# One softmax over both head groups for three of four batches, and a newly searched order of the first stage

## The chip, the core and the metric

The kernel runs on one core of a Trainium2 chip (trn2). The metric is the device time of one execution in microseconds; the kernel before took 826.61 us (median of 3 runs, 824.13 to 828.91).

## The reference

Three blocks follow each other. All inputs and the output are float32, but for the five weight matrices, which are float64.

```
# attention through 32 memory slots, 4 batches, 8 heads, 576 positions, head size 64
a      = softmax(phi over the 576 positions)           # [4,8,576,32]
k_m    = a^T k ;  v_m = a^T v                          # [4,8,32,64]
scores = q k_m^T / 8 ; attn = softmax(scores over 32)  # [4,8,576,32]
x      = (attn v_m) laid out as [2304, 512]
# first feed-forward block, 512 -> 2048 -> 512
x      = silu(x w_in) w_out
# second, 512 -> 1536 -> 512
out    = ((x w_a) * (x w_b)) w_out2
```

Nearly all products are made three times over: a float32 operand is split into a high part and a low part (what is left), and high by high, low by high and high by low are added up.

## The kernel before

**Stage one, 0 to about 131 us.** For each batch b the steps are: `weights` (L628), the softmax of phi up to its exp `ex`; `memory` (L655), 144 small products `kvp` of `ex` with k and v, their division `kvn` on ScalarE, and k_m transposed (`kt`, copied to `kT`); `values` (L700), v_m transposed (`vt`); `turn` (L709), q transposed, three turns of three 128x128 transposes (`qt`, copied to `qT` by ScalarE) for each of two head groups; and `scores` (L743), for each head group: eight products into the one `sc` tile, two VectorE transposes into `x`, the softmax over 32 slots (maximum, subtraction, exp on ScalarE, sum, division), a transpose back into `xt`, and the split of `xt` into the high part `at` (ScalarE) and the low part. `vw_first` (L873) folds v_m into w_in (`mp`, split into `m0` to `m3` by batch), so that the first product of the feed-forward block is `hp` = m times at, and the second `yp` = g times w_out with g = silu(hp). `tile_of` (L796) turns a float64 tile of w_in or w_out into float32 by integer operations. The feed-forward units of batches 0, 1 and half of 2 (`UNITS`, L910) run in this stage too, between the attention steps.

Each of these steps is a generator that says, by `op` (L531), which engine it needs, for how many ns by its author's table, after what, and which ring of buffers it takes. `run` (L571) plays that through: it takes the step of the lowest rank in the table `R` (L956) among those that can start, and issues it. So each engine gets a fixed order, in which it waits where its next instruction isn't ready. `keep_busy` (L236) puts products of ones, which nobody reads, into the bank about to be used, where the plan sees TensorE idle. The loads go out on SyncE's queue in the order of `LOADS` (L948): a name is the tensor, the batch and the head group (q20 is q of batch 2, head group 0; kv31 is k and v of batch 3, head group 1; wi and wo are tiles of w_in and w_out). A load waits until its buffer is free; q, kv and phi have two buffers each, weight tiles three, so the queue stands still behind a load that waits. `LOW_A` (L953) says how the low half of `at` is made, by batch: "V" is a subtraction on VectorE; "D" is a negated copy on ScalarE and a DMA from GpSimd that adds `xt`.

**Stage two, to about 405 us,** is the rest of the first feed-forward block, in the order of a scheduler that does not keep the program's order. **Stage three** is the second block in seven products a step (Strassen's scheme); its operands `yq` are split from y and from differences `T` of blocks of y (`sums`, L1092; `quarter_task`, L1110), in an order by the same `run`. PSUM has eight banks; each stage allocates pools of them, and the next stage's pools take the same banks: before, y and h's pools came first, then t (`bank`) and sc.

```
            t["x"] = p_s.tile([128, 2 * J, NM], F32, tag="x", bufs=2, name="x")
            t["xt"] = p_s.tile([128, 2, S], F32, tag="x", bufs=2, name="xt")
```

x and xt of a batch share that ring of two, so batch b + 1's scores can be taken into x only when batch b's x has been transposed.

Of the kernel before, what the change touches and what calls it, by code (L numbers as in the profile page):

```python
# [20 lines left out]
def attn_moe_moe2_kernel(  # L21
# [457 lines left out]
    ff["h"] = tc.alloc_tile_pool(name="ps_h", bufs=2, space=PSUM)
    ps_t = tc.alloc_tile_pool(name="ps_t", bufs=2, space=PSUM)  # L480
    ps_sc = tc.alloc_tile_pool(name="ps_sc", bufs=1, space=PSUM)
# [474 lines left out]
    R = dict(  # L956
        weights=(6, 55, 5, 16), memory=(26, 2, 43, 9), values=(46, 19, 22, 54), turn0=(38, 14, 15, 33),
        turn1=(24, 48, 41, 45), scores0=(7, 36, 47, 37), scores1=(23, 59, 28, 18), vw=(51, 53, 44, 49),
        first=(3,), m0=(4, 39, 11, 50), m1=(8, 32, 27, 35), wi=(12, 17, 31, 57), wo=(56, 1, 29, 21),
        units=(40,), g=(10,), y=(58,), late0=(20, 25, 34, 0), late1=(30, 52, 13, 42),  # L960
    )
# [385 lines left out]
```

## Time and profile before

| | us |
|---|---|
| median of 3 runs | 826.61 |
| the profiled execution | 829.91 |
| its span, first to last instruction | 828.1 |
| TensorE (PE) busy | 802.7, 97% of the span |
| VectorE (DVE) busy | 534.6, 65% |
| ScalarE (ACT) busy | 438.8, 53% |
| mean granted TensorE clock | 0.987 |

A granted clock of 1.00 is 2.4 GHz, 0.50 is 1.2 GHz, so the mean says how much of the span ran at half speed. PE's matmuls overlap, so its busy time is no measure of speed, but a gap in it is time in which no matmul ran.

### The profile page before, as it was taken

To read this page: it belongs to the slowest core of one execution; us is meant where nothing else is said; L and a number is where in the kernel's file an instruction comes from. 1 tells how busy PE (TensorE), PEld (TensorE's weight loads), DVE (VectorE), ACT (ScalarE), POOL (GpSimd) and SP (SyncE) were. 2 spreads that over 40 slices of the span, in tenths; PEclk is the share of its full clock that TensorE was granted. 3 is DMA by queue.
4 is the path that set the end of the run, shared out by engine and by line. 5 is a ranking of instruction groups with operands and counts; after the bars stand their busy time and mean duration, and the time that the engine had idled before them with its cause. 6 is when DMAs were issued, how large, how long until landed. Compare 5 with 4: busy or idle time off the path is not lost.

```text
span 828.1 us, 14335 instructions
## 1 busy us (share of the span) xinstructions
PE 802.7 (97%) x5696; PEld 737.4 (89%) x5696; DVE 534.6 (65%) x1050; ACT 438.8 (53%) x891; POOL 60.6 (7%) x75
## 2 busy tenths in 40 slices
PE   8888979999999999999999999999999999999997
PEld 5567869899999999999899999999999999999996
DVE  6887766656646665667698886568655685452534
ACT  4675677854654565667367765554424643222220
POOL 1000000100000000112001100110000100000000
PEclk9999999999999999999999999999999999999999
DMA  9757022432231232446397679877785975757753
GB/s 345 271 190 276 2 56 83 122 77 79 64 64 51 78 77 51 97 116 127 142 351 207 205 256 312 256 223 250 228 238 169 277 225 154 212 167 201 214 144 77
DMA packets 59027, 139.42 MB, mean 168 GB/s; under 512 B 5072, under 2 KB 30160, under 8 KB 58960
## 3 DMA queue, kind: packets, MB, share of 16 engines
q1 hardware_dynamic: 48448, 122.44, 44.2%
q0 software_dynamic: 9360, 15.54, 11.1%
q8 instruction: 45, 0.74, 0.4%
q10 hardware_dynamic: 1152, 0.52, 0.3%
q14 instruction: 22, 0.18, 0.1%
HBM read 101.71 MB, written 21.23 MB: 148 GB/s over the span
## 4 chain that ended last, share of the span: by engine, by line
PE 83%; DVE 1%; DMA 1%; ACT 0%; issue 0%
PE ab L69 31%; PE yp L69 22%; PE op L69 18%; PE hp L69 11%; PE mp L69 2%; DMA st_b<-in_moe_w_b_dram 1%; DVE yq L69 0%; DVE T L69 0%; ACT yq L69 0%; DVE y L69 0%; ACT y L69 0%; ACT u L69 0%; DVE e_a L78 0%; ACT e_b L78 0%
## 5 line engine op out<-in xcount | busy, mean ns | idle before, releaser
L69 PE MATMUL ab<-yq,wh 128*128 128x384 f32 x1080 | 260.3, 338 | 2.0 <-DVE yq L69 1.2
L69 PEld LDWEIGHTS ab<-yq,wh 128*128 128x128 f32 x1080 | 196.6, 189 | 9.2 <-DVE yq L69 1.5
L69 PE MATMUL ab<-yq,wl 128*128 128x384 f32 x432 | 146.1, 338 | 0.0
L69 DVE TENSOR_TENSOR gl<-g,gh 128x288 fp32r<-128x288 f32 x128 | 58.1, 455 | 66.6 <-ACT gh L69 66.4
L69 ACT ACTIVATE g<-hp 128x288 f32<-128x288 f32 x128 | 52.5, 410 | 86.7 <-PE hp L69 80.4
L69 ACT ACTIVATE u<-ab 128x384 f32<-128x384 f32 x108 | 52.4, 490 | 86.3 <-PE ab L69 85.7
L69 DVE TENSOR_TENSOR y<-op,y 128x512 f32<-128x512 f32 x54 | 37.3, 691 | 77.8 <-PE op L69 76.9
L69 PE MATMUL op<-wol,ph 128*128 128x512 f32 x216 | 85.4, 395 | 0.0
L69 PE MATMUL op<-woh,pl 128*128 128x512 f32 x216 | 85.1, 394 | 0.0
L69 PE MATMUL op<-woh,ph 128*128 128x512 f32 x216 | 84.3, 390 | 0.0
L69 PEld LDWEIGHTS ab<-yq,wl 128*128 128x128 f32 x432 | 81.5, 189 | 0.0
L69 DVE TENSOR_TENSOR u<-ab,u 128x384 f32<-128x384 f32 x108 | 59.8, 555 | 20.5 <-PE ab L69 19.5
L69 ACT ACTIVATE ph<-u 128x384 fp32r<-128x384 f32 x72 | 37.4, 524 | 67.0 <-DVE u L69 59.0
L69 DVE TENSOR_TENSOR y<-yp,y 128x288 f32<-128x288 f32 x104 | 47.3, 456 | 28.4 <-PE yp L69 28.2
L69 ACT ACTIVATE gh<-g 128x288 fp32r<-128x288 f32 x128 | 56.6, 443 | 3.1
L69 PEld LDWEIGHTS op<-woh,pl 128*128 128x128 f32 x216 | 40.5, 188 | 8.9
L69 PEld LDWEIGHTS op<-woh,ph 128*128 128x128 f32 x216 | 40.6, 188 | 6.7
L69 PEld LDWEIGHTS op<-wol,ph 128*128 128x128 f32 x216 | 40.5, 188 | 6.7
L69 PE MATMUL yp<-gh,wo_0h 128*128 128x288 f32 x128 | 39.0, 305 | 5.5 <-ACT y L69 4.5
L69 DVE TENSOR_TENSOR pl<-u,ph 128x384 fp32r<-128x384 f32 x72 | 39.2, 551 | 2.0 <-ACT ph L69 1.8
L69 PE MATMUL yp<-gh,wo_2h 128*128 128x288 f32 x128 | 38.9, 304 | 0.0
L69 PE MATMUL yp<-gl,wo_1h 128*128 128x288 f32 x128 | 38.2, 298 | 0.0
(175 smaller groups left out, 1734.9 us busy)
## 6 DMA issues: line engine op xcount, KB each, us to landing
yq<-yd SPq DMA_DIRECT2D x63, 768.0 KB, 4.5
yd<-yq SPq DMA_DIRECT2D x21, 768.0 KB, 4.3
st_wo<-in_moe_w_out_dram SPq DMA_DIRECT2D x16, 512.0 KB, 3.5
st_wi<-in_moe_w_in_dram SPq DMA_DIRECT2D x16, 512.0 KB, 5.1
st_a<-in_moe_w_a_dram SPq DMA_DIRECT2D x12, 512.0 KB, 5.3
st_b<-in_moe_w_b_dram SPq DMA_DIRECT2D x12, 512.0 KB, 5.3
wl<-s POOLq DMA_DIRECT2D x24, 256.0 KB, 5.8
st_o<-in_moe_w_out_dram SPq DMA_DIRECT2D x12, 512.0 KB, 6.0
```

Source lines behind the costliest of these rows:

```text
L69: ins = f(*a, **k)
```

## The change

For batches 1, 2 and 3 (`JOINT`), `scores` stops after its transposes into `x`, and a new generator `softmax` waits for both head groups and does each softmax operation once on [128, 36, 32] in place of twice on [128, 18, 32]; `split_at` then splits each head group's half of `xt`. The low half of batch 3 is made on VectorE. `LOADS`, the ranks `R` and the banks for `weights` and `turn` are new, found by a search over the plan (a load that the plan sees idle for over 1 us counts 1.5 us more in it, and `vw_first` waits in it for the batch before). The PSUM pools of all three stages are put in another order. In stage three, the first differences `T` get 1 us later in the plan.

```diff
+            if eng == "D" and at - free_at["D"] > 1000.0:
+                at += 1500.0
...
+        if b in JOINT:
+            if hg == 1:
+                add(R["soft"][b], softmax(b), free_at["T"])
+            return
...
+    def softmax(b):
+        yield op("V", 1370, [f"tx{b}0", f"tx{b}1"], take=("mxq", f"mxq{b}"))
+        x = st[b]["x"]
+        full = [128, 2 * J, NM]
+        mx = p_s.tile([128, 2 * J], F32, tag="mxq", bufs=2, name="mxq")
+        V.tensor_reduce(out=mx, in_=x, op=ALU.max, axis=AX.X)
+        yield op("V", 1360, free=[f"mxq{b}"])
+        V.tensor_tensor(out=x, in0=x, in1=mx.unsqueeze(2).to_broadcast(full), op=ALU.subtract)
+        yield op("A", 1180, table="exp")
+        A.activation(out=x, in_=x, func=AF.Exp, scale=scale)
+        yield op("V", 1900, take=("smq", f"smq{b}"))
+        sm = p_s.tile([128, 2 * J], F32, tag="smq", bufs=2, name="smq")
+        V.tensor_reduce(out=sm, in_=x, op=ALU.add, axis=AX.X)
+        V.tensor_scalar_add(sm, sm, EPS)
+        V.reciprocal(out=sm, in_=sm)
+        yield op("V", 1360, free=[f"smq{b}"])
+        V.tensor_tensor(out=x, in0=x, in1=sm.unsqueeze(2).to_broadcast(full), op=ALU.mult)
+        yield op("V", 1400, take=("x", f"xt{b}"), done=f"xt{b}", free=[f"x{b}"])
+        xt = st[b]["xt"] = p_s.tile([128, 2, S], F32, tag="x", bufs=2, name="xt")
+        V.transpose(out=xt.rearrange("p g s -> p (g s)"), in_=x.rearrange("p j m -> p (j m)"))
+        for g in range(2):
+            add(R["halves"][b], split_at(b, g), free_at["T"])
+    def split_at(b, g):
+        yield op("A", 680, [f"xt{b}"])
+        xt = st[b]["xt"][:, g]
+        hi, lo = at_hi[b][g], at_lo[b][g]
+        copy(A, hi, xt)
+        for o in low_half(LOW_A[b], 740, 680, hi, lo, xt, f"at{b}{g}0", f"xt{b}*2"):
+            yield o
...
-        "phi00 phi10 wo01 wo02 wi00 kv00 kv01 wi01 wi03 q01 wo00 q00 kv11 wi02 q11 kv10 q10 q21 q20 kv21 "
-        "phi20 kv20 wo03 kv30 kv31 q31 phi30 q30 "
+        "phi00 phi10 wi00 wo01 kv00 wo00 kv01 wi03 q00 wi01 q01 kv10 q11 kv11 wo03 phi20 q21 phi30 q10 kv21 "
+        "wi02 kv20 q31 q20 wo02 kv31 kv30 q30 "
...
-    LOW_A = ("V", "V", "V", "D")
+    LOW_A = ("V", "V", "V", "V")
...
+    JOINT = (1, 2, 3)
...
+        ps_o = mctx.enter_context(tc.tile_pool(name="ps_o", bufs=2, space=PSUM))
         ps_x = mctx.enter_context(tc.tile_pool(name="ps_x", bufs=WG, space=PSUM))
         ps_z = mctx.enter_context(tc.tile_pool(name="ps_z", bufs=WG, space=PSUM))
-        ps_o = mctx.enter_context(tc.tile_pool(name="ps_o", bufs=2, space=PSUM))
...
-            add(due_quarter(NS * tp + 2), sums(tp))
+            add(due_quarter(NS * tp + 2), sums(tp), 0.0 if tp else 1000.0)
```

The other pools move in the same way: stage one allocates t, h, sc, y in place of y, h, t, sc, and stage two m, h2, y2 in place of y2, h2, m. So `ps_x`, which stage three writes first, takes the banks of h2 and not those of y2.

**SyncE's loads, from the first q of batch 1 on.** `qq` is a load of q, `kv0` and `kv1` are the two buffers of k and v, `ph` is phi, `st_wo3` and `st_wi2` are weight tiles. Before (`qq_417` is q11, `qq_481` q10, `qq_575` q21, `qq_639` q20):

```order
L69 DMA qq_417<-in_q_dram 128x1x1152
L69 DMA kv1_116<-in_k_dram 128x2x576
L69 DMA kv1_116<-in_v_dram 128x2x576
L69 DMA qq_481<-in_q_dram 128x1x1152
L69 DMA qq_575<-in_q_dram 128x1x1152
L69 DMA qq_639<-in_q_dram 128x1x1152
L69 DMA kv0_115<-in_k_dram 128x2x576
L69 DMA kv0_115<-in_v_dram 128x2x576
L69 DMA ph_694<-in_phi_dram 128x4x288
L69 DMA kv1_116<-in_k_dram 128x2x576
L69 DMA kv1_116<-in_v_dram 128x2x576
L69 DMA st_wo3_752<-in_moe_w_out_dram 128x512
```

and with the change (`qq_391` is q11, `qq_558` q21, `qq_574` q10):

```order
L69 DMA qq_391<-in_q_dram 128x1x1152
L69 DMA kv1_116<-in_k_dram 128x2x576
L69 DMA kv1_116<-in_v_dram 128x2x576
L69 DMA st_wo3_450<-in_moe_w_out_dram 128x512
L69 DMA ph_478<-in_phi_dram 128x4x288
L69 DMA qq_558<-in_q_dram 128x1x1152
L69 DMA ph_562<-in_phi_dram 128x4x288
L69 DMA qq_574<-in_q_dram 128x1x1152
L69 DMA kv0_115<-in_k_dram 128x2x576
L69 DMA kv0_115<-in_v_dram 128x2x576
L69 DMA st_wi2_626<-in_moe_w_in_dram 128x2x256
L69 DMA kv1_116<-in_k_dram 128x2x576
```

The phi loads of batches 2 and 3 and tile 3 of w_out now stand ahead of q10. Before, q10 followed k and v of batch 1 at once, and phi of batch 3 stood near the end of the list, between its two q.

**ScalarE at the end of stage one,** around the split of batch 3's `at` and the copies of the last `yp` into y. Before:

```order
L69 ACTIVATE at_74<-xt 128x576
L69 ACTIVATE e_wi_0_1621<-st_wi_0_1440 128x512
L69 ACTIVATE g_1689<-hp 128x288
L69 ACTIVATE gh<-g_1689 128x288
L69 ACTIVATE at_82<-at_74 128x576
L69 ACTIVATE m3h<-mp 128x512
L69 ACTIVATE at_73<-xt 128x576
L69 ACTIVATE at_81<-at_73 128x576
L69 ACTIVATE m3h<-mp 128x512
L69 ACTIVATE y_123<-yp 128x288 x2
L69 ACTIVATE y_1732<-yp 128x288
```

and with the change:

```order
L69 ACTIVATE at_73<-xt 128x576
L69 ACTIVATE g_1634<-hp 128x288
L69 ACTIVATE gh<-g_1634 128x288
L69 ACTIVATE g_1647<-hp 128x288
L69 ACTIVATE gh<-g_1647 128x288
L69 ACTIVATE e_wi_0_1624<-st_wi_0_1482 128x512
L69 ACTIVATE at_74<-xt 128x576
L69 ACTIVATE y_123<-yp 128x288 x2
L69 ACTIVATE g_1714<-hp 128x288
L69 ACTIVATE g_1749<-hp 128x288
L69 ACTIVATE gh<-g_1714 128x288
L69 ACTIVATE gh<-g_1749 128x288
```

The two negated copies (`at_82<-at_74`, `at_81<-at_73`) are gone, `m3h` has moved ahead, and the last two copies into `y_123` no longer stand behind three `at` copies and two `m3h`.

**VectorE where stage three starts** (the `y` rows add stage two's last `yp` to y). Before:

```order
L78 ISA t_o_5246<-t_o_5246,e_o_5216 128x1024
L69 TENSOR_TENSOR y_1732<-yp,y_1732 128x288 x6
L69 TENSOR_TENSOR T_5428<-y_123 128x768
L69 TENSOR_TENSOR yq<-y_123,yq 128x768 x2
L69 TENSOR_TENSOR T_5440<-y_123,T_5428 128x768
L69 TENSOR_TENSOR T_5442<-y_123 128x768
```

and with the change:

```order
L78 ISA t_o_5214<-t_o_5214,e_o_5184 128x1024
L69 TENSOR_TENSOR y_1703<-yp,y_1703 128x288 x6
L69 TENSOR_TENSOR yq<-y_123,yq 128x768 x2
L69 TENSOR_TENSOR T_5406<-y_123 128x768
L69 TENSOR_TENSOR T_5408<-y_123,T_5406 128x768
L69 TENSOR_TENSOR T_5414<-y_123 128x768
```

The low halves of the first two operands `yq` now come ahead of the first difference `T`.

## Rows read from the trace of the kernel before

**Rows 1.** Stretches: length, busy us of PE, PEld, DVE, ACT, POOL; clock; DMA share; GB/s.
```profile
0.00:72.85 72.85, 61.23 (x871) 44.58 (x872) 58.42 (x120) 48.51 (x99) 3.27 (x10) 0.98 0.72 258
72.85:131.25 58.40, 51.06 (x538) 45.39 (x537) 36.96 (x77) 36.99 (x74) 1.87 (x2) 0.88 0.25 83
131.25:404.60 273.35, 273.34 (x2131) 260.11 (x2129) 169.54 (x362) 166.53 (x366) 23.42 (x27) 1.00 0.33 83
404.60:412.00 7.40, 5.54 (x21) 5.32 (x22) 7.33 (x9) 2.15 (x3) 0.00 (x0) 0.77 0.61 246
412.00:823.60 411.60, 411.44 (x2141) 382.06 (x2139) 261.65 (x484) 184.62 (x349) 32.09 (x36) 1.00 0.73 221
```

**Rows 2.** Timeline of PE at four places and where stage three starts: start, length, waits.
```profile
72.85 0.43 PE L69 MATMUL hp<-at,m1h 128*128 128x288 f32 x2
...
80.16 2.15 PE L69 MATMUL qt<-ident,qq 128*128 128x128 f32 x8 [2.74 <-DMA qq<-in_q_dram]
...
121.10 0.61 PE L69 MATMUL yp<-gh,wo_0h 128*128 128x288 f32 x1 [4.34 <-ACT y L69]
...
131.25 0.43 PE L69 MATMUL hp<-at,m3h 128*128 128x288 f32 x2
...
406.87 0.46 PE L69 MATMUL ab<-yq,wh 128*128 128x384 f32 x1 [1.23 <-DVE yq L69]
```

**Rows 3.** Timeline of ACT just before PE goes on at 121.10.
```profile
119.28 0.68 ACT L69 ACTIVATE at<-at 128x576 fp32r<-128x576 f32 x1
120.35 0.70 ACT L69 ACTIVATE y<-yp 128x288 f32<-128x288 f32 x2
```

**Rows 4.** Stretches of one us around two falls of the clock (columns as in rows 1).
```profile
21.00:22.00 1.00, 0.87 (x7) 0.80 (x7) 0.97 (x3) 0.53 (x3) 0.00 (x0) 1.00 1.05 415
...
23.00:24.00 1.00, 0.10 (x1) 0.00 (x0) 0.07 (x1) 0.77 (x2) 0.00 (x0) 1.00 1.04 389
...
25.00:26.00 1.00, 1.00 (x9) 0.67 (x8) 0.97 (x3) 0.65 (x3) 0.00 (x0) 0.50 1.05 390
...
80.00:81.00 1.00, 0.84 (x4) 0.87 (x5) 0.97 (x4) 0.00 (x0) 0.00 (x0) 0.50 1.03 410
```

**Rows 5.** The stretch 10 to 20 us, and the PE row that waited for v.
```profile
10.00:20.00 10.00, 8.29 (x166) 4.81 (x164) 8.87 (x16) 6.10 (x9) 0.00 (x0) 1.00 1.05 395
...
16.40 3.13 PE L69 MATMUL kvp<-kv,ex 64*32 64x192 f32 x136 [1.23 <-DMA kv<-in_v_dram]
```

**Rows 6.** Groups by line and shape up to 131.25 us: xcount | busy us, mean ns.
```profile
L69 DVE TENSOR_TENSOR x<-x,mxq 128x576 f32<-128x576 f32 x8 | 6.1, 757 | 0.2
...
L69 DVE TENSOR_TENSOR ex<-ph,bc 128x1152 f32<-128x1152 f32 x4 | 5.4, 1349 | 0.9 <-PE bc L69 0.9
...
L69 DVE STREAM_TRANSPOSE xt<-x 128x576 f32<-128x576 f32 x8 | 6.2, 776 | 0.2
...
L69 DVE TENSOR_TENSOR at<-xt,at 128x576 fp32r<-128x576 f32 x6 | 4.4, 736 | 0.0
...
L69 ACT ACTIVATE qT<-qt 128x384 f32<-128x384 f32 x24 | 11.1, 490 | 5.3 <-PE qt L69 5.2
...
L69 ACT ACTIVATE ex<-ex 128x1152 f32<-128x1152 f32 x4 | 4.7, 1164 | 0.6 <-DVE ex L69 0.6
```

**Rows 7.** Timeline of PE: products of ones, and attention products at full clock.
```profile
9.36 5.34 PE L69 MATMUL kvp<-ones 128*128 128x512 bf16 x24
...
93.40 3.15 PE L69 MATMUL kvp<-kv,ex 64*32 64x192 f32 x144
...
103.02 0.82 PE L69 MATMUL qt<-ident,qq 128*128 128x128 f32 x6
...
113.10 1.09 PE L69 MATMUL mp<-wi,vt 64*32 64x256 f32 x32
```

**Rows 8.** Timeline of DVE where stage three starts.
```profile
405.00 0.95 DVE L69 TENSOR_TENSOR T<-y 128x768 f32<-128x768 f32 x1
405.87 1.82 DVE L69 TENSOR_TENSOR yq<-y,yq 128x768 fp32r<-128x768 f32 x2
```

More of the change, by code (lines that the diff above doesn't have):

```diff
@@ L477, in attn_moe_moe2_kernel @@
     p_c = tc.alloc_tile_pool(name="p_c", bufs=1, side="right")
+    ps_t = tc.alloc_tile_pool(name="ps_t", bufs=2, space=PSUM)
+    ff["h"] = tc.alloc_tile_pool(name="ps_h", bufs=2, space=PSUM)
+    ps_sc = tc.alloc_tile_pool(name="ps_sc", bufs=1, space=PSUM)
     ff["y"] = tc.alloc_tile_pool(name="ps_y", bufs=2, space=PSUM)
[L479 to L481 removed]
     mm_pool[:] = ps_t, "t"
@@ L760, in scores @@
                 T.matmul(sc[o, par, :k], t["kT"][r, hg, o], qT[r, i0:i1, 32 * p : 32 * p + 32])
-        yield op("V", 150 + 780 * nj / J, [f"xt{b - 1}"] if b else [], take=("x", f"x{b}"), free=[f"sc{key}"])
+        yield op("V", 150 + 780 * nj / J, [f"xt{b - 1}"] if b else [], take=("x", f"x{b}"), done=f"tx{b}{hg}", free=[f"sc{key}"])
         if "x" not in t:
@@ L878, in vw_first @@
         yield op("T", 100 + 470 * len(halves), [f"vbd{b}"] + [f"wi{2 * hf + kc}" for hf in halves for kc in range(2)]
-                 + [f"{key}_0"] * halves[0], done=f"{key}_{halves[0]}", take=takes, rec=32 * len(halves))
+                 + [f"{key}_0"] * halves[0] + [f"m{b - 1}_{int(b == 1)}"] * (b > 0), done=f"{key}_{halves[0]}", take=takes, rec=32 * len(halves))
         cols = slice(256 * halves[0], 256 * halves[-1] + 256)
@@ L948, in attn_moe_moe2_kernel @@
     LOADS = (
-        "phi00 phi10 wo01 wo02 wi00 kv00 kv01 wi01 wi03 q01 wo00 q00 kv11 wi02 q11 kv10 q10 q21 q20 kv21 "
-        "phi20 kv20 wo03 kv30 kv31 q31 phi30 q30 "
+        "phi00 phi10 wi00 wo01 kv00 wo00 kv01 wi03 q00 wi01 q01 kv10 q11 kv11 wo03 phi20 q21 phi30 q10 kv21 "
+        "wi02 kv20 q31 q20 wo02 kv31 kv30 q30 "
     ).split()
     CUT = ()
-    LOW_A = ("V", "V", "V", "D")
+    LOW_A = ("V", "V", "V", "V")
     LOW_O = ("V", "V", "V", "V")
     BANKS = ("bank", "hp", "yp", "sc")
+    JOINT = (1, 2, 3)
     R = dict(
[L957 to L960, printed above, removed]
+        weights=(34, 57, 28, 60), memory=(26, 0, 7, 17), values=(54, 36, 35, 52), turn0=(49, 64, 30, 58),
+        turn1=(20, 12, 10, 48), scores0=(25, 39, 33, 4), scores1=(32, 56, 62, 41), vw=(24, 65, 53, 42),
+        first=(47,), m0=(40, 27, 43, 23), m1=(11, 21, 63, 16), wi=(15, 19, 61, 55), wo=(50, 37, 6, 66),
+        units=(51,), g=(8,), soft=(5, 29, 46, 13), halves=(45, 67, 14, 18), y=(22,), late0=(44, 59, 9, 31),
+        late1=(2, 38, 1, 3),
     )
-    BANK_W = ("yp", "yp", "yp", "yp")
+    BANK_W = ("yp", "hp", "bank", "hp")
     BANK_K = ("bank", "sc", "sc", "bank")
-    BANK_Q = ("bank", "yp", "yp", "hp")
+    BANK_Q = ("yp", "yp", "hp", "yp")
     fill()
@@ L988, in attn_moe_moe2_kernel @@
     pinned[0] = False
-    for p in (ps_sc, ps_t, ff["h"], ff["y"], p_c, p_s, p_in):
+    for p in (ff["y"], ps_sc, ff["h"], ps_t, p_c, p_s, p_in):
         p.release()
+    ps_m = tc.alloc_tile_pool(name="ps_m", bufs=2, space=PSUM)
+    ff["h"] = tc.alloc_tile_pool(name="ps_h2", bufs=3, space=PSUM)
     ff["y"] = tc.alloc_tile_pool(name="ps_y2", bufs=3, space=PSUM)
-    ff["h"] = tc.alloc_tile_pool(name="ps_h2", bufs=3, space=PSUM)
     p_y2 = ctx.enter_context(tc.tile_pool(name="p_y2", bufs=1, side="right"))
@@ L1017, in attn_moe_moe2_kernel @@
         tick()
-    for p in (p_g2, p_m2, ps_m, ff["h"], ff["y"], p_g, p_t, p_a):
+    for p in (p_g2, p_m2, ff["y"], ff["h"], ps_m, p_g, p_t, p_a):
         p.release()
```

1 line of the change is left out of this document (removed).

## The prediction

> **What bounds the kernel now.** I read the busy times by stretch first [rows 1]. From 131.25 us to 404.6 TensorE is busy for 273.34 of 273.35 us at a granted clock of 1.00, and from 412 to 823.6 for 411.44 of 411.60. The products there stay the same, so nothing can be gained in them: the other engines have room and would have to become much slower to be seen. Time can be won only in stage one, around 405 us, and in the end. Stage one has two parts. Up to 72.85 us, where the first `hp` of batch 1 stands [rows 2], TensorE waits for loads and for the softmax chain, and fills up with products of ones. From there to 131.25, the first `hp` of batch 3, it is idle for 58.40 - 51.06 = 7.34 us, and the mean clock is 0.88. The timeline of TensorE tells where [rows 2]: 2.74 us before a `qt` that waits for a load of q, and 4.34 us before a `yp` that waits for ScalarE's copy into y. What ScalarE did just before is in its own timeline [rows 3]: the negated copy of batch 3's `at` ran at 119.28, and the two copies out of `yp` that TensorE waited for came only after it, at 120.35. Behind such gaps the clock is at 0.50, 1.2 GHz, as in 80 to 81 us [rows 4]. A mean of 0.88 is 0.12 x 58.40 = 7.0 us of full-speed time not granted, of which I take 0.6 to have fallen into the idle time; 6.4 us were lost by slow products, 3.2 a gap. So the stretch holds 7.3 + 6.4 = 13.7 us of loss, and 58.4 - 13.7 = 44.7 us of work.
>
> **The two losses go.** With the change every `qt` stands ahead of the first `hp` of batch 1 in TensorE's order, the wait for q with it. The ScalarE copies into y follow one `at` copy, and the two negated copies, 0.68 us each [rows 3], don't exist. Neither place has anything left that TensorE would wait for, if the engines get there in time. That is 13.7 us less, against what the earlier part now costs.
>
> **The earlier part: more work ahead of the first hp of batch 1.** By the order, TensorE has done more by then: one more `kvp` set (3.15 us), two more sets of nine `qt` (0.82 for six, so 2.5 for both), one more `mp` (1.09), two more `sc` (half as many products each as `mp`, a little wider: 1.2), and eight more 128-column products of the `qt` kind at 0.14, 1.1, all by [rows 7]: 9.0 us together. The stretch after it shrinks by as much, to 44.7 - 9.0 = 35.7. If nothing else changed, the first `hp` of batch 1 would stand at 72.85 + 9.0 = 81.9.
>
> When will it stand there? I follow the chain that I take to set it. It begins with q10, which now has phi of batches 2 and 3 and a tile of w_out ahead of it. Up to and with it the queue holds 4 loads of phi, 5 of q, 8 of k or v (576 KB each, by the tiles' shapes) and 6 weight tiles (512 KB), 13.17 MB. The v that TensorE awaited at 16.40 [rows 5] ends 5.11 MB in both lists. The other 8.06 MB at 395 GB/s [rows 5] take 20.4 us: q10 lands at 36.8. Three transposes and three `qT` copies of 0.49 [rows 6] end at 38.7. ScalarE's exp of batch 0's second head group stands behind them, 0.68 by its sister of the same shape [rows 3]: 39.4. VectorE's sum, division and transpose back, with small operations between, take 3.0 [rows 6]: 42.4. The subtraction for `ex` of batch 2 follows (1.35), its exp (1.16) and a `qT` copy (0.49), after which TensorE gets its bank: 45.4. Five products of ones at 0.22, twelve `hp` products at 0.14, like `qt`'s, and the third `kvp` at 3.15 [rows 7] follow: 51.4, and VectorE's reciprocal ends at 51.9. From that one to the low half of batch 1's `at`, on which the first `hp` of batch 1 waits, VectorE has 49 instructions. Seven of 1152 columns at 1.35, one transpose of 1152 at 1.45 and two low halves of `at` at 0.74 make 12.4 us [rows 6]; the other 39, conversions of weights, score transposes, low halves of g, additions into y, cost 0.17 to 0.69 each in the same view, 17.5 together: 29.9. With 2 us of waits inside (for the last `kvp`, for ScalarE's half of w_out's tiles), an estimate, the first `hp` of batch 1 stands at 84.0, 2.1 us later than the 81.9.
>
> **The joint softmax** itself is nearly free of effect. Per head group the old form has four operations of 576 columns at about 0.757 and a transpose of 0.776 [rows 6], 7.61 us per batch. An operation of 1152 columns costs 1.349 in the one row that has that size, and at most twice 0.757; I take the row, and 1.45 for the transpose, between 1.349 and twice 0.776: 6.85 us. That is 0.76 us a batch, and 0.4 more for the small ones; three batches give 3.5. Batch 3's low halves put 1.5 us back on VectorE and take 1.4 off ScalarE. Its cost is delay: the first maximum waits for the second head group's transposes, and behind it in VectorE's order stand low halves of g and m0, for which `yp` and `hp` of batch 0 wait. The work that covers it is the attention of the next batches on TensorE; where that ran out, each batch would pay the first group's 3.8 us. Tile 2 of w_in and of w_out move too, behind k and v of batch 2 and q20: w_out's last tiles are ready only near the end of those 49 instructions, so four `yp` come after them. They are part of the work counted, not more of it.
>
> **After the first hp of batch 1** 35.7 us of work remain, and 1.3 us of short waits, an estimate, where `yp` banks and `mp` of batch 3 meet a busy VectorE: batch 3's first `hp` at 121.0, 10.2 us earlier than 131.25. The cover needed: VectorE must have finished the low half of m3 by then. Counted in the same way that is 28.5 us of work behind the 29.9, 58.4 from 51.9 on, so a busy share of 0.85.
>
> **The clock in the new order.** TensorE will stand idle twice, from about 34 to 37 (for q10, with four products of ones ahead) and from 42 to 45 (for the bank). Before, three short gaps cost it the full clock: it worked 0.87 us in 21 to 22 and 0.10 in 23 to 24, and was at 0.50 by 25 [rows 4]. The price is nothing at the one end and at the other both gaps: 3.2 us for one like that at 80 us and 1.5 for one like that at 25 us (a mean of 0.98 over 72.85 us [rows 1]), 4.7. I take the middle, 2.4, since there is one such gap for each. The Trainium skill ("TensorE: Matmul & The Clock Gate", Part 1) says that the half rate comes after at least one idle window. Matmuls ran in each of the microseconds shown before 25, so the trace doesn't agree; by that rule neither gap, with products of ones in or near it, need cost anything, and the sum would be 2.4 us lower, 815.5 for the median.
>
> **Around 405 us** `ab` waits 1.23 us for VectorE's `yq` [rows 2], ahead of which stood a difference T of 0.95 us, 0.87 from its start to that of `yq` [rows 8]. It now stands behind. The pool `ps_x` also moves off the banks of the last `yp`, but its second product waits for the same `yq`, so this alone wins nothing. Gain 0.9; if the clock also held (0.77 over 7.40 us [rows 1]), 1.7 more; if something else were late there, nothing. I take 0.9. The other pool moves cost no instruction and I cost them at nothing; what hides them is that all copies out of the old banks end before, and if one didn't, that is a copy of some 0.4 us (two take 0.70 [rows 3]).
>
> **Sum.** 829.91 - 10.2 + 2.4 - 0.9 = 821.2 for an execution like the profiled one. That one was 3.3 us above the median of 826.61, so **817.9 us** for the median.
>
> **Rivals.**
> *The clock holds* in both gaps and at 405 us: 2.4 + 1.7 less, 813.8. Against it stand [rows 4]. The Trainium skill's rule named above would make this the likelier case.
> *The loads come late* (still faster or the same). For q10, 317 GB/s in place of 395 would bring it 5 us later, and up to the first `hp` of batch 1 all is one chain, so the whole delay counts: 822.9. For it: every buffer of q has to come free before, so few loads are in flight. Against it: the queue is never empty in 10 to 20 us.
> *VectorE becomes the bound.* In the old stage one it was busy for 0.80 of the first 72.85 us and 0.63 of the next 58.4 [rows 1], always with waits for another engine; here it needs 0.85. Its order is fixed, so a wait for a late `kvp` or exp holds all behind it: the tile conversions, then `at`, `gl`, m3. With a share s the first `hp` of batch 3 stands at 51.9 + 58.4/s. At 0.80 that is 124.9, some 819; from 0.77 to 0.69 it gives back the gain to within 4.1 us of the median; below 0.69 the kernel is **slower** than before by over 0.5%. At 0.65, 141.7: ten later than before, 836. Against it: the waits of the old 72.85 to 131.25 were mostly those two gaps of TensorE.
>
> **Chances.** Half a per cent, 4.1 us, is what a measurement of this kernel can tell from no change. My forecast 0.60, clock holds 0.13 (faster both); loads late by 5 us or more 0.13 and VectorE at 0.69 to 0.77 0.07 (both within 0.5%); VectorE below 0.69, 0.07 (slower). Faster 0.73, same 0.20, slower 0.07. The range: down to 811 for a held clock and fewer waits than I put in, up to 826 for late loads or a VectorE share of 0.73.
>
> **What would show it.** Right: no `qt` wait for q after 65 us; no gap of TensorE over 2 us after the first `hp` of batch 1, which stands at 84 to 87; the first `hp` of batch 3 at 119 to 124; clock 1.00 from there; the wait for `yq` where stage three starts at 0.4 us or less, or its pair of gaps shorter by 0.5 us; TensorE waiting 2 us or more for q10 near 35. Wrong: a gap in which `mp` or `hp` waits for VectorE's m or `at` for several us, the clock at 0.50 between 85 and 120, or a first `hp` of batch 1 after 90.

## The result, and the profile after

| | before | changed |
|---|---|---|
| median, us | 827.24 (4 runs, 824.13 to 828.91) | 814.59 (4 runs, 814.25 to 815.25) |
| ratio | | 0.9852, 95% interval 0.9822 to 0.9883 |
| profiled execution, us | 829.91 | 814.76 |
| its span, us | 828.1 | 812.9 |
| mean granted clock | 0.987 | 0.998 |

The change made the kernel faster by 12.65 us (1.5%). The forecast was 817.9 us with a range of 811 to 826: the direction and the range held, and the gain was 4 us larger than the 8.7 that the forecast made against its median of 826.61.

The stretches of the changed kernel that answer to [rows 1] (columns as there; the first hp of batch 1 stands at 81.52, the last yp ends at 389.65):

```profile
0.00:81.52 81.52, 71.88 (x1108) 52.39 (x1111) 65.59 (x127) 56.26 (x112) 3.27 (x10) 0.98 0.76 275
81.52:116.55 35.03, 35.03 (x298) 33.07 (x291) 28.64 (x49) 27.53 (x57) 0.00 (x0) 1.00 0.05 17
116.55:389.65 273.10, 273.10 (x2139) 260.98 (x2137) 169.77 (x363) 167.21 (x367) 23.56 (x27) 1.00 0.33 83
389.65:397.05 7.40, 6.16 (x35) 5.99 (x35) 7.28 (x9) 2.07 (x3) 0.00 (x0) 1.00 0.61 251
397.05:812.90 415.85, 409.05 (x2127) 379.51 (x2125) 262.50 (x485) 184.59 (x348) 32.06 (x36) 1.00 0.72 219
```

From 81.52 to 389.65 us TensorE has no idle time that the view shows, at a clock of 1.00. Its timeline at the places of [rows 2], and at two new ones in stage three:

```profile
35.84 0.88 PE L69 MATMUL qt<-ident,qq 128*128 128x128 f32 x6 [0.29 <-DMA qq<-in_q_dram]
...
46.90 3.25 PE L69 MATMUL kvp<-kv,ex 64*32 64x192 f32 x144 [1.85 <-DVE wi L69]
...
81.52 0.54 PE L69 MATMUL hp<-at,m1h 128*128 128x288 f32 x2
...
116.55 0.43 PE L69 MATMUL hp<-at,m3h 128*128 128x288 f32 x2
...
391.06 0.44 PE L69 MATMUL ab<-yq,wh 128*128 128x384 f32 x1 [1.24 <-DVE yq L69]
...
400.00 0.62 PE L69 MATMUL ab<-yq,wh 128*128 128x384 f32 x2 [1.54 <-ACT u L69]
...
404.35 0.62 PE L69 MATMUL ab<-yq,wh 128*128 128x384 f32 x2 [0.81 <-ACT u L69]
```

The q10 that the forecast put at 36.8 us is used at 35.84. The first `hp` of batch 1 stands at 81.52 and that of batch 3 at 116.55 (forecast 84.0 and 121.0). The single wait for `yq` is 1.24 us, and two waits for `u` have come that the kernel before did not have. All of TensorE's waits up to 140 us, by what was waited for (total, times, longest):

```profile
PE qt L69 <- ACT qT L69: 3.6, 4, 2.1
PE kvp L69 <- DVE wi L69: 1.9, 1, 1.9
PE bc L69 <- ACT mb L69: 1.0, 1, 1.0
...
PE qt L69 <- DMA qq<-in_q_dram: 0.6, 2, 0.3
PE kvp L69 <- DMA kv<-in_v_dram: 0.4, 1, 0.4
```

In the list as a whole neither the 2.74 us for q at 80 us nor the 4.34 us for ScalarE's copies into y is there. Clock in stretches of one us, for [rows 4]:

```profile
24.00:25.00 1.00, 1.00 (x12) 0.64 (x18) 0.58 (x2) 1.00 (x3) 0.00 (x0) 0.50 1.15 207
45.00:46.00 1.00, 0.04 (x1) 0.00 (x0) 0.93 (x3) 1.00 (x3) 0.00 (x0) 1.00 1.03 406
46.00:47.00 1.00, 0.10 (x4) 0.13 (x9) 0.93 (x4) 0.98 (x2) 0.00 (x0) 1.00 0.98 399
390.00:391.00 1.00, 0.00 (x0) 0.00 (x0) 1.00 (x3) 0.00 (x0) 0.00 (x0) 1.00 0.00 0
391.00:392.00 1.00, 0.94 (x5) 0.94 (x6) 1.00 (x3) 0.00 (x0) 0.00 (x0) 1.00 0.23 92
```

Up to the end of the span the clock is at 0.50 near 24 us only, behind a wait of 2.15 us. In 45 to 47 us, where TensorE worked 0.14 us of two, and in 390 to 391, where it did nothing, it stayed at 1.00. The joint softmax's prices, for [rows 6]:

```profile
L69 DVE TENSOR_TENSOR x<-x,mxq 128x1152 f32<-128x1152 f32 x3 | 4.0, 1350 | 0.0
...
L69 DVE STREAM_TRANSPOSE xt<-x 128x1152 f32<-128x1152 f32 x3 | 4.1, 1375 | 0.1
```

### The profile page after: what moved, and what is told of

It is laid out like the page before. It is cut to its first block, busy times and chain, and to the rows that moved or that the text cites. A ratio compares the mean times of both kernels' runs of the same rounds, so it can differ in the third digit from the quotient of the medians.

```text
span 812.9 us, 14300 instructions
## 1 busy us (share of the span) xinstructions
PE 795.2 (98%) x5693; PEld 731.9 (90%) x5696; DVE 533.8 (66%) x1031; ACT 437.7 (54%) x886; POOL 58.9 (7%) x73
## 4 chain that ended last, share of the span: by engine, by line
PE 93%; DMA 3%; DVE 2%; ACT 1%; SPq 1%; issue 0%; ACTq 0%
PE ab L69 31%; PE yp L69 25%; PE op L69 18%; PE hp L69 13%; PE mp L69 2%; PE kvp L69 2%; DMA st_wo<-in_moe_w_out_dram 1%; DMA kv<-in_v_dram 1%; DMA st_b<-in_moe_w_b_dram 1%; SPq L69 1%; DVE yq L69 0%; PE qt L69 0%; PE sc L69 0%; DVE x L69 0%; DVE m L69 0%
## 5 line engine op out<-in xcount | busy, mean ns | idle before, releaser
L69 PE MATMUL yp<-gh,wo_2l 128*128 128x288 f32 x128 | 37.9, 296 | 0.0
```

The costliest lines, as they stand in the source:

```text
L69: ins = f(*a, **k)
```

## The experiments

Theory: TensorE's two gaps in stage one and their half clock are the gain; ScalarE's negated copies make the second gap; the pool order and the joint form count for nothing. Rivals: the pool order makes the second gap; the joint form gives the gain by itself; the clock costs what gaps cost. All medians are set against the kernel before in the same comparison (826.58, 827.33 and 826.74 us in the three of them).

| kernel | median us | less than before | ratio (95%) |
|---|---|---|---|
| x1_low_v | 824.96 | 1.62 | 0.9985 (0.9972 to 0.9997) |
| x2_pools | 821.93 | 4.65 | 0.9945 (0.9929 to 0.9961) |
| x3_ones | 826.49 | 0.09 | 1.0001 (0.9991 to 1.0012) |
| z1_q_early | 824.61 | 2.13 | 0.9976 (0.9965 to 0.9986) |
| z2_q_pools_sums | 819.37 | 7.37 | 0.9909 (0.9893 to 0.9925) |
| x4_halves | 814.72 | 11.86 | 0.9872 (0.9853 to 0.9892) |
| y1_no_ones | 816.16 | 11.17 | 0.9868 (0.9851 to 0.9885) |
| y2_old_pools | 818.32 | 9.01 | 0.9894 (0.9879 to 0.9909) |
| y3_u_first | 820.98 | 6.35 | 0.9931 (0.9917 to 0.9945) |
| y4_wi2_early | 815.63 | 11.70 | 0.9860 (0.9843 to 0.9876) |
| z3_u_later_conv | 813.53 | 13.21 | 0.9846 (0.9828 to 0.9864) |
| z4_no_joint | 834.56 | -7.82 | 1.0095 (1.0076 to 1.0115) |

The first five start from the kernel before, the others from the changed one. The intervals of x4_halves, y1_no_ones, y2_old_pools, y4_wi2_early and z3_u_later_conv overlap with that of the changed kernel (0.9822 to 0.9883), so differences of a few us among these go by the medians alone, where no trace is named for them.

**x1_low_v and x2_pools: what makes the 4.34 us gap?**

```diff
-    LOW_A = ("V", "V", "V", "D")
+    LOW_A = ("V", "V", "V", "V")
```

> Kernel before, with the low half of batch 3 made by a subtraction on VectorE; loads, ranks, softmax and pools stay. Theory (the prediction's): the 4.34 us stall before a yp is ScalarE's negated copies of at, 0.68 us each, ahead of the copies into y, and the half clock behind it costs 3.2 us; VectorE gets two subtractions of 0.74. So the stall at 121 goes, and the time falls by 4 to 7.5 us (ratio 0.991 to 0.995). Rival: the stall is set by something else (the banks that the new pool of yp takes over), and it stays within 1 us: ratio 0.998 to 1.002.

```diff
-    ff["y"] = tc.alloc_tile_pool(name="ps_y", bufs=2, space=PSUM)
-    ff["h"] = tc.alloc_tile_pool(name="ps_h", bufs=2, space=PSUM)
     ps_t = tc.alloc_tile_pool(name="ps_t", bufs=2, space=PSUM)
+    ff["h"] = tc.alloc_tile_pool(name="ps_h", bufs=2, space=PSUM)
     ps_sc = tc.alloc_tile_pool(name="ps_sc", bufs=1, space=PSUM)
+    ff["y"] = tc.alloc_tile_pool(name="ps_y", bufs=2, space=PSUM)
...
-    ff["y"] = tc.alloc_tile_pool(name="ps_y2", bufs=3, space=PSUM)
+    ps_m = tc.alloc_tile_pool(name="ps_m", bufs=2, space=PSUM)
     ff["h"] = tc.alloc_tile_pool(name="ps_h2", bufs=3, space=PSUM)
+    ff["y"] = tc.alloc_tile_pool(name="ps_y2", bufs=3, space=PSUM)
...
-    ps_m = tc.alloc_tile_pool(name="ps_m", bufs=2, space=PSUM)
...
+        ps_o = mctx.enter_context(tc.tile_pool(name="ps_o", bufs=2, space=PSUM))
         ps_x = mctx.enter_context(tc.tile_pool(name="ps_x", bufs=WG, space=PSUM))
         ps_z = mctx.enter_context(tc.tile_pool(name="ps_z", bufs=WG, space=PSUM))
-        ps_o = mctx.enter_context(tc.tile_pool(name="ps_o", bufs=2, space=PSUM))
```

> Kernel before, with the PSUM pools of all three stages in the changed order and nothing else. Theory (the prediction's): the pool order costs and brings nothing; the 4.34 us stall at 121 stays, and the time is the same within 1 us (ratio 0.999 to 1.001). Rival: the yp that stalls there is the first tile of the new pool of stage two, which takes over the banks of the last yp of stage one and so waits for their copies into y; in the changed order it takes other banks, so the stall and its half clock go, 4 to 7.5 us (ratio 0.991 to 0.995), and the late copies on ScalarE hurt nobody.

The first `yp` of stage two, in x1_low_v, with ScalarE's copies ahead of it (timeline of all engines):

```profile
115.44 1.07 ACT L69 ACTIVATE m3h<-mp 128x512 fp32r<-128x512 f32 x2
...
116.39 0.71 ACT L69 ACTIVATE y<-yp 128x288 f32<-128x288 f32 x2
...
117.16 0.61 PE L69 MATMUL yp<-gh,wo_0h 128*128 128x288 f32 x1 [2.23 <-ACT y L69]
```

and in x2_pools:

```profile
115.36 0.69 ACT L69 ACTIVATE at<-at 128x576 fp32r<-128x576 f32 x1
...
115.93 0.60 ACT L69 ACTIVATE m3h<-mp 128x512 fp32r<-128x512 f32 x1
...
116.41 0.73 ACT L69 ACTIVATE y<-yp 128x288 f32<-128x288 f32 x2
...
117.19 0.40 PE L69 MATMUL yp<-gh,wo_0h 128*128 128x288 f32 x1 [0.20 <-ACT y L69]
...
396.91 0.44 PE L69 MATMUL ab<-yq,wh 128*128 128x384 f32 x1 [2.10 <-DVE yq L69]
```

Without the negated copies the wait is 2.23 us, half of what it was, and the time falls by 1.6 us: less than the theory's 4 to 7.5, more than the rival's 1. With the pools in the new order, and both negated copies still ahead of the copies into y, the wait is 0.20 us (after 0.63 for `m3h` just ahead of it) and the time falls by 4.65. The rival holds: before, the new pool's first banks were those of the last `yp` of stage one, so its first tile had to wait for ScalarE's copies out of them. In x2_pools the order of TensorE also differs there (the scheduler put `hp` ahead of that `yp`, as no bank held it up), and that is part of the same effect.

**y2_old_pools: the same the other way round.** The diff is that of x2_pools, reversed, on the changed kernel.

> Changed kernel with the PSUM pools of all three stages in the order of before. Theory (the prediction's): the pool order counts for nothing, and the time is that of the changed kernel within 0.5 us (ratio to before 0.985). Rival: the first yp of stage two then takes over the banks of the last yp of stage one and waits for ScalarE's copies into y, and the first product of stage three waits for VectorE's last addition into y (0.64 us before): 1 to 5 us more (ratio 0.986 to 0.991).

```profile
112.77 0.40 PE L69 MATMUL yp<-gh,wo_0h 128*128 128x288 f32 x1 [1.86 <-ACT y L69]
...
394.20 0.41 PE L69 MATMUL ab<-yq,wh 128*128 128x384 f32 x1 [0.65 <-DVE y L69]
394.98 0.45 PE L69 MATMUL ab<-yq,wh 128*128 128x384 f32 x1 [0.36 <-DVE yq L69]
```

A wait of 1.86 us for ScalarE's copies returns, although the negated copies are gone and `m3h` stands earlier, and the time is 3.7 us above the changed kernel's. The ratios' intervals overlap a little, but none of its four executions (817.77 to 819.14) comes near the changed kernel's (814.25 to 815.25). So the pool order is worth 4.65 us from the one side and 3.7 from the other, and the prediction costed it at nothing.

**z1_q_early and x3_ones: the gap at 80 us.** In z1_q_early the load of q31 is issued ahead of that of k and v of batch 3, in `loads`:

```diff
                 kv = st[b]["kv", hg] = kv_t[n_kv[0] % 2]
+                if (b, hg) == (3, 0):
+                    qq = st[3]["qq", 1] = p_in.tile([128, J * D], F32, tag="qq", bufs=2, name="qq")
+                    Y.dma_start(out=qq, in_=q[3].rearrange("(x g) (i j) d -> g i x (j d)", g=2, i=32)[1])
...
+                if (b, hg) == (3, 1):
+                    continue
```

> Kernel before, with the load of q of batch 3, head group 1, issued ahead of k and v of batch 3 instead of behind them; every engine keeps its order. Theory (the prediction's): the 2.74 us wait of a qt at 80 us and the half clock behind it, 3.2 us, go, and TensorE reaches batch 3 2.7 to 5.9 us earlier: ratio 0.993 to 0.9967. Rival: the wait goes, but the time won is lost again in the 4.34 us stall at 121 us, which ScalarE's chain of copies sets and not TensorE: within 1 us of before (0.999 to 1.001).

In x3_ones, ten products of ones ahead of the first `qt` of batch 3's second head group:

```diff
+        if (b, hg, n) == (3, 1, 0):
+            spare[0] = 10
         qt = bank_of(BANK_Q[b], "qt")[:, :384].rearrange("p (i s) -> p i s", i=3)
```

> Kernel before, with ten products of ones in the bank of the qt that waits 2.74 us for a load of q at 80 us. Theory (the prediction's): the gap costs its own 2.74 us and 3.2 us by the half clock behind it; the products fill the gap, the wait for q stays, the clock stays at 1.00 in 80 to 85 us, and the time falls by 2 to 3.2 us (ratio 0.996 to 0.9975). Rival: the half clock there is hidden behind later waits for other engines, or the clock falls in spite of the products: same within 1 us (0.999 to 1.001).

Moving the load cut the wait to 0.38 us and brought 2.13 us, below the 2.7 that was the least the theory gave. The gap of 4.34 us behind it stayed. The load moved is not the one that this `qt` waits for: at 80 us the first head group of batch 3 is turned, and q30 is the last load in the queue. Without q31 between, q30 was sent off at 66.28 us in place of 68.91.

The ten products of x3_ones therefore stand in the wrong place, as its timeline shows:

```profile
78.59 0.85 PE L69 MATMUL qt<-ident,qq 128*128 128x128 f32 x6 [1.71 <-DMA qq<-in_q_dram]
...
100.54 2.33 PE L69 MATMUL qt<-ones 128*128 128x512 bf16 x10
102.71 0.82 PE L69 MATMUL qt<-ident,qq 128*128 128x128 f32 x6
```

They ran 20 us behind the gap, ahead of the `qt` of q31. TensorE stayed idle before the waiting `qt`, and the clock fell behind it:

```profile
80.00:81.00 1.00, 1.00 (x7) 0.93 (x6) 1.00 (x3) 0.52 (x2) 0.00 (x0) 0.51 0.38 152
```

So the unchanged time says nothing on what such products in the gap would do to the clock. The gap itself differs from one execution to the next. In x1_low_v and x2_pools, with the same loads, it is

```profile
80.52 0.84 PE L69 MATMUL qt<-ident,qq 128*128 128x128 f32 x6 [2.22 <-DMA qq<-in_q_dram]
```

and

```profile
77.91 0.85 PE L69 MATMUL qt<-ident,qq 128*128 128x128 f32 x6 [1.49 <-DMA qq<-in_q_dram]
```

and the clock stayed at 1.00 behind both, which is why closing it brings less than 2.74 us and a half clock.

**z2_q_pools_sums: do the parts add up?** It is z1_q_early, x2_pools and the one line of `sums` on the kernel before.

> Kernel before, with three things: the load of q as in the run on it alone, the changed order of the PSUM pools, and the later first differences T of stage three; loads otherwise, ranks and softmax as before. Theory: both gaps of TensorE in stage one go with their half clock, and the gap where stage three starts gets shorter; with the pools' 4.7 us as measured, 2.7 to 5.9 for q and 0.9 for T the time falls by 8.3 to 11.5 us (ratio 0.986 to 0.990), which leaves 1 to 4 us of the changed kernel's 12.7 to the new search, the joint softmax and the subtraction on VectorE. Rival: without the new order VectorE or ScalarE is late for what follows, the gains do not add up, and the time falls by 5 to 6 us (ratio 0.993 to 0.994).

It is 7.37 us faster: 2.13 for q and 4.65 for the pools leave 0.6 for the later T, which was not run alone. Within intervals of about 1.3 us either way the parts add up. By the profiles the later T gives less than 0.6: from the last `yp` to the end of the span it takes 423.5 us in x2_pools and 423.2 here. The sum lies between the two numbers that were expected: above the rival's 5 to 6, and below the theory's 8.3, as q brought less than 2.7. TensorE from 62 us to the end of its last `yp`, by the same view of stretches in each kernel:

| kernel | stretch, us | PE busy, us | idle, us |
|---|---|---|---|
| before | 62.00 to 404.59 | 335.25 | 7.34 |
| z1_q_early | 62.00 to 398.76 | 331.54 | 5.22 |
| x2_pools | 62.00 to 394.62 | 329.61 | 3.01 |
| z2_q_pools_sums | 62.00 to 394.46 | 330.88 | 1.58 |
| changed | 62.00 to 389.65 | 327.65 | 0.00 |

The 4.8 us between z2_q_pools_sums and the changed kernel belong to the new search, the joint softmax and the subtraction for batch 3 together, which were not run one by one. In the profiled executions 1.58 us is this idle time, and 3.23 is TensorE work (330.88 less 327.65, both at a clock of 1.00) that the changed kernel has behind it by 62 us: three sets of `kvp` where z2_q_pools_sums has done two, for fewer `hp` and `yp`.

**x4_halves and z4_no_joint: the joint form.** In x4_halves each operation stands twice, in the same place:

```diff
-        V.tensor_reduce(out=mx, in_=x, op=ALU.max, axis=AX.X)
+        for h in HJ:
+            V.tensor_reduce(out=mx[:, h], in_=x[:, h], op=ALU.max, axis=AX.X)
```

and so on for the others, `HJ` being the two halves.

> Changed kernel, the same order on every engine, but each operation of the joint softmax issued as two of half its width, one after the other in its place: 3.5 us more of VectorE work in all, 1.2 us a batch. Theory (the prediction's): the joint form has nearly no direct effect on the time; with TensorE without waits after 62 us, the extra work is hidden but for the part in front of the first hp of batch 1, 1.2 us for batch 1's softmax, and the time is 0 to 1.2 us above the changed kernel (ratio to before 0.985 to 0.987). Rival: VectorE's chain sets both the first hp of batch 1 and that of batch 3, and all of the 3.5 us shows (ratio 0.989).

```diff
-    JOINT = (1, 2, 3)
+    JOINT = ()
```

> Changed kernel with the softmax of every batch per head group as before, planned with the same ranks, so the order changes behind 45 us. Theory: the joint form itself brings little; loads, pools and the removal of the two gaps stay, and the time is 0 to 3.5 us above the changed kernel (ratio to before 0.985 to 0.989). Rival: the joint form is what lets VectorE keep up, and without it a wait for at, m or x of several us returns: 5 us or more above the changed kernel (ratio over 0.991).

The work itself costs nothing that shows: 814.72 against 814.59, within what the theory gave. The ratios alone would not settle it, as the interval reaches to the rival's 0.989; but in the trace the first `hp` of batch 1 stands at 81.31 and that of batch 3 at 116.31, no later than in the changed kernel. Without the joint form and with the same ranks the kernel is 20 us slower than the changed one, and slower than before (timeline of all engines):

```profile
109.22 0.78 DVE L69 STREAM_TRANSPOSE xt<-x 128x576 f32<-128x576 f32 x1
110.04 0.68 ACT L69 ACTIVATE at<-xt 128x576 fp32r<-128x576 f32 x1 [2.55 <-DVE xt L69]
...
111.03 1.21 PE L69 MATMUL sc<-qT,kT 64*32 64x288 f32 x16 [8.16 <-DVE x L69]
```

TensorE waits 8.16 us for one `sc`, whose tile the transposes into x had to free, and they stood behind the second head group's transposes into `xt` (x and xt share two buffers). TensorE is idle for 8.88 us from 62 us to its last `yp`, the clock is at 0.50 for 107 to 117 us, and the plan put in 39 more products of ones. So the size is the rival's. What the joint form changed, by these two runs, is the order that comes out of the ranks, and with it when the shared buffers come free, not the work. The ranks were searched with it; whether a search without it would end as well wasn't tried.

**y1_no_ones and y4_wi2_early: the part up to 50 us.** In y1_no_ones `keep_busy` issues nothing behind 30 us of the plan.

```diff
+        if spare[0] and quiet[0] and free_at["T"] > 30000.0:
+            spare[0] = 0
         for _ in range(spare[0]):
...
+    quiet[0] = 3
```

> Changed kernel without its eleven products of ones after 30 us, the same order otherwise. Theory (the one the prediction took for its sum): short gaps cost the clock, and it holds in 34 to 48 us only because products of ones stand in the gaps; without them it falls to 0.50 once or twice, 1.5 to 4.7 us of slow products, of which 0.5 to 2.4 us reach the end (ratio to before 0.986 to 0.988). Rival: what holds the clock is the work in between, products of ones or not; the clock stays at 1.00 there and the time is that of the changed kernel within 0.5 us (ratio 0.985).

In stretches of one us:

```profile
46.00:47.00 1.00, 0.00 (x0) 0.00 (x0) 0.93 (x4) 0.98 (x3) 0.00 (x0) 0.50 1.03 417
...
48.00:49.00 1.00, 1.00 (x38) 1.00 (x30) 0.20 (x2) 0.97 (x3) 0.00 (x0) 0.50 0.86 343
```

The clock was at 0.50 from 46 to 52 us, the first `hp` of batch 1 stood at 84.41, and the median is 1.6 us more: within the theory. That the products of ones hold the clock is not shown by it. The execution profiled is the slowest of four (817.76 us); the fastest took 814.76 at a mean clock of 0.998, like the changed kernel. And y3_u_first, below, has the products and the same order there, and its clock fell all the same at 46 us.

In y4_wi2_early the load of tile 2 of w_in goes out ahead of k and v of batch 2:

```diff
+                if (b, hg) == (2, 1):
+                    s64 = st["w"]["wi2"] = p_w.tile([128, W], U64, tag="st", bufs=3, name="st_wi2")
+                    Y.dma_start(out=s64.rearrange("p (a b) -> p a b", a=2),
+                                in_=w_in[0:256, 256:512].rearrange("(a p) n -> p a n", p=128))
                 kv = st[b]["kv", hg] = kv_t[n_kv[0] % 2]
...
+                if name == "wi2":
+                    continue
```

> Changed kernel, with the load of tile 2 of w_in issued ahead of k and v of batch 2, head group 1; all other engines keep their order. Theory: up to 47 us the loads bound the stage, and the third kvp waits for the last of k and v, whose place in the queue hardly moves; ScalarE's wait of 1.32 us for the tile goes, and the time stays within 0.5 us (ratio to before 0.985). Rival: the chain over ScalarE and VectorE bounds it, as the profile's name for the 1.85 us wait says (wi on VectorE); kvp comes 1.3 us earlier and the time falls by up to 1.3 us (ratio 0.9835).

It took 1.0 us more, so neither held to its number. There was no gain, against the rival, but the profiled execution is no clean comparison: a `qt` waited 2.48 us for q at 29.79, and the clock was at 0.50 from 32 to 35 and from 42 to 45 us, where the changed kernel's was at 1.00. In z3_u_later_conv, with the changed kernel's order up to 50 us, the same wait of the third `kvp` has the name of a load:

```profile
46.62 1.67 PE L69 MATMUL kvp<-kv,ex 64*32 64x192 f32 x68 [1.82 <-DMA kv<-in_v_dram]
```

So it has in y1_no_ones, y2_old_pools and y3_u_first (1.75, 2.52 and 2.11 us). In these four it waits for v; that the name wi in the changed kernel's own row is a coincidence in time is likely by them, but not shown.

**y3_u_first and z3_u_later_conv: the new waits for u.** ScalarE in the changed kernel:

```profile
398.91 0.66 ACT L78 ACTIVATE e_a<-st_a 128x512 uint32<-128x512 uint32 x1 [3.04 <-DVE t_a L78]
399.47 0.86 ACT L69 ACTIVATE u<-ab 128x384 f32<-128x384 f32 x2
...
403.26 0.67 ACT L78 ACTIVATE e_b<-st_b 128x512 f32<-128x512 f32 x1 [1.08 <-DMA st_b<-in_moe_w_b_dram]
403.83 0.85 ACT L69 ACTIVATE u<-ab 128x384 f32<-128x384 f32 x2
```

Its copies of u, for which TensorE waits, stand behind a conversion's copies that wait for VectorE (3.04 us) and for a load (1.08). The first edit plans the whole conversion of that tile later, the second only its second copy, and the next tile's conversion:

```diff
-            add(at, weight_f32(n, x))
+            add(at, weight_f32(n, x), 12000.0 if n == WG and x == "a" else 0.0)
```

> Changed kernel, with the conversion of the first weight tile of stage three planned some us later, so that ScalarE's first copies of u stand ahead of it. Theory: the two waits for u at 400 and 404 us (1.54 and 0.81 us), which the kernel before did not have, come from ScalarE waiting for VectorE inside that conversion; they go, and the time falls by 1.5 to 2.3 us below the changed kernel (ratio to before 0.982 to 0.983). Rival: another wait takes their place, for yq or for u, and the time is that of the changed kernel within 0.5 us.

```diff
-            yield op("V", 700)
+            yield op("V", 700, wait=3000.0 if n == WG and x == "a" else 100)
             f["signed"](x)
...
-            add(at, weight_f32(n, x))
+            add(at, weight_f32(n, x), {"a": 0.0, "b": 18000.0}.get(x, 0.0) if n == WG else 0.0)
```

> Changed kernel, with one conversion's second copy on ScalarE planned 3 us later and the next weight tile's conversion later too, so that the first three copies of u, and two of the next three, stand ahead of them; less is moved than in the run that put the whole first conversion behind. Theory: the waits of 1.54 and 0.81 us for u go and no new one comes, so the time is 1.5 to 2.3 us below the changed kernel (ratio to before 0.982 to 0.983). Rival: another load or conversion is late in their place, as in that run, and the time is the changed kernel's or more (ratio 0.985 or more).

The timeline of y3_u_first:

```profile
405.25 0.66 ACT L78 ACTIVATE e_b<-st_b 128x512 f32<-128x512 f32 x1 [4.75 <-DMA st_b<-in_moe_w_b_dram]
...
406.35 1.01 PE L69 MATMUL ab<-yq,wh 128*128 128x384 f32 x2 [3.32 <-ACT u L69]
```

It lost 6.4 us against the changed kernel: both waits went, but the next copies of u stood behind a load awaited for 4.75 us, TensorE waited 3.32 us for them, and the clock was at 0.50 from 405 to 411 us and, behind a wait of 2.39 us for `yq`, from 463 to 466. z3_u_later_conv, TensorE alone:

```profile
390.76 0.45 PE L69 MATMUL ab<-yq,wh 128*128 128x384 f32 x1 [1.24 <-DVE yq L69]
...
400.44 0.62 PE L69 MATMUL ab<-yq,wh 128*128 128x384 f32 x2 [0.18 <-ACT u L69]
...
404.12 0.61 PE L69 MATMUL ab<-yq,wh 128*128 128x384 f32 x2 [1.33 <-ACT u L69]
```

The first wait is down to 0.18 us, the second is 1.33, behind the same load, for which ScalarE waits 2.27 us. The median is 1.06 us below the changed kernel's, the fastest kernel here, less than the theory's 1.5, and its interval overlaps with that of the changed one.

## Why the prediction was right, and where it was not

**Both gaps went, as forecast; the cause of the second was wrong.** "The ScalarE copies into y follow one at copy, and the two negated copies don't exist" was taken for the reason. x1_low_v shows that this halves the wait and brings 1.6 us; x2_pools and y2_old_pools show that the PSUM pools decide it, 4.65 and 3.7 us. The step that failed is "The other pool moves cost no instruction and I cost them at nothing", with a copy of 0.4 us as its bound: the waiting instruction was the first tile of stage two's pool, and what it waited for was the row of [rows 3] that the prediction itself read, two copies out of `yp`. The first gap was mis-sized: 2.74 us and 3.2 for its half clock were those of one execution, which was 2.7 us above its median. In x1_low_v, x2_pools and x3_ones the wait was 2.22, 1.49 and 1.71 us, and the clock fell behind the last only; z1_q_early brought 2.13 us in the medians. In the profiled executions it was 5.8 us up to the last `yp` (404.59 to 398.76), but 1.1 of them lie ahead of the first `hp` of batch 1 (72.85 to 71.75), where the load had no part. That the second gap went is luck as far as the prediction goes: by the step that it gave, a wait of 1.86 us would have stayed, and the kernel would have taken the 818.32 us of y2_old_pools, which lies nearer to the forecast than the time of the changed kernel.

**The chain to the first hp of batch 1** was 2.5 us too long, 0.2 of it an error in the sum: 51.9 + 29.9 + 2 is 83.8, not 84.0. q10 was used at 35.84 us in place of 36.8, TensorE got its bank earlier than at 45.4 (`hp` at 42.6), VectorE's reciprocal ended at 50.57 in place of 51.9, and from there to the end of batch 1's last low half of `at`, 81.05, passed 30.5 us, near the 29.9 + 2, though in other parts: VectorE was busy for 27.24 us of it and idle for 3.24. Three other executions of the same order had that `hp` at 81.21 to 82.94, so part of this is their spread. VectorE was busy for 53.53 of the 62.36 us from there to the end of batch 3's m, a share of 0.86. The forecast had 58.4 us of work there at a share of 0.85, so the work was put 4.9 us too high. The rival of VectorE as the bound didn't come. Three of the signs of being right did not come: the first `hp` of batch 1 at 84 to 87 (81.52), that of batch 3 at 119 to 124 (116.55), and a wait of 2 us for q10 (0.29).

**The joint softmax** was forecast as "nearly free of effect" in its work, and x4_halves bears that out; the sizes taken, 1.35 and 1.45, measured 1.35 and 1.38. That its ranks and the joint form belong together (z4_no_joint) was in no step.

**The clock** was the term in the wrong place: an allowance of 2.4 us was added for two gaps near 36 and 44 us, and neither brought the clock down in the changed kernel's profiled execution. That is the rival in which the clock holds, 813.8 us, within 0.8 of the result. Why it held stays open: without the products of ones it fell in y1_no_ones, with them it fell in y3_u_first. The Trainium skill ("TensorE: Matmul & The Clock Gate", Part 1) has the half rate come after at least one idle window; by that rule the sum would have been 815.5 us, nearer than the one taken. At these two gaps the trace of the changed kernel agrees, the clock being at 1.00; that of the kernel before does not where stage three starts, where the clock fell with a product of 0.41 us between two gaps.

**Around 405 us** the forecast's 0.9 us was there and did not count. From the end of the last `yp` to the product that waits for `yq` it took 2.28 us before (404.59 to 406.87) and takes 1.41 now (389.65 to 391.06), and the clock held as well, for which 1.7 us were priced. But from the same end to the end of the span it took 423.51 us before and 423.25 after: 0.3 us. What took the rest back is a path that the step has only as "if something else were late there, nothing": VectorE's and a load's, over ScalarE's conversion copies, behind which the copies of u stand. Before:

```profile
413.72 0.66 ACT L78 ACTIVATE e_a<-st_a 128x512 uint32<-128x512 uint32 x1 [2.98 <-DVE t_a L78]
...
418.29 0.68 ACT L78 ACTIVATE e_b<-st_b 128x512 f32<-128x512 f32 x1 [0.92 <-DMA st_b<-in_moe_w_b_dram]
```

That is 9.13 and 13.70 us behind the end of the last `yp`; the same two copies of the changed kernel, at 398.91 and 403.26, stand 9.26 and 13.61 behind it. So ScalarE came no earlier, and TensorE's lead was lost. Counted from the same end, the 38th product of stage three starts at 11.73 us before and 8.47 now, 3.26 earlier; behind the two waits for u the 62nd starts at 17.03 and 16.72. The longer gap and the slow products of the kernel before had hidden these copies. In all five kernels where the clock fell at that place (before, x1_low_v, x2_pools, x3_ones, z1_q_early) the waits for u are 0.2 us or nothing; in seven where it held they are 2.3 to 2.5 us, and y3_u_first and z3_u_later_conv moved the copies. The five also have the earlier T, so no run parts the slow clock's share in the hiding from that of T.

**The sum.** By the profiled executions TensorE ended stage two 14.9 us earlier (404.59 to 389.65), where 10.2 less 2.4 was forecast; of those 14.9 some 2.7 are the profiled execution's own distance from its median. Against the profiled execution the sum, 821.2, was 6.4 us above the 814.76: the clock's 2.4, the first chain's 2.5, 2.0 behind it (35.7 and 1.3 forecast, 35.03 taken), less 0.6 at 405 us. In the medians the error is half of that, since the changed kernel's profiled execution is 0.2 us above its median, not 3.3. That is luck too: the 3.3 us taken off for one execution's distance from its median offset half of what the other terms were too high.

## What to carry to other kernels

When a stage ends and its PSUM pools are freed, ask which bank the first tile of the next stage takes over and which copy empties it last: here the order of pool allocation alone was worth about a third of the gain, though it adds no instruction and takes none away. Suspect a bank handover first where a stall stands ahead of the first tile of a pool. After a gap is closed, look for the next engine's copies, which may come no earlier than before: here ScalarE's conversion copies stood 9.1 us behind the last `yp` before and 9.3 after, and the gain ahead of them was lost.

## What was not expected of the hardware

Where stage three starts, one gap of 1.24 us never brought the clock down in a profiled execution (eight kernels: the changed one, x4_halves, y1_no_ones, y3_u_first, y4_wi2_early, z2_q_pools_sums, z3_u_later_conv, z4_no_joint), while 0.64 + 1.23 us with 0.41 us of work between (before, x1_low_v, x3_ones, z1_q_early) and 2.10 us in one (x2_pools) always did. With 0.65 and 0.36 us (y2_old_pools) it held. In stage one a gap of near the same length in the same order went both ways: the clock held in the changed kernel at 45 to 47 us (1.85 us before the `kvp`) and fell in y3_u_first there (2.11 us), while in y2_old_pools it held at 2.52. At 80 us it held behind waits of 2.22 and 1.49 us for q (x1_low_v, x2_pools) and fell behind 1.71 and 2.74 (x3_ones, before). So in this kernel a gap of about 2 us is a risk to the clock rather than a price.
